# A hand-scheduled spectral + GLU kernel: the planner's assumed durations and two lags are changed, and with them the order of instructions

## Chip, cores, metric

One core of one Trainium2 chip. The metric is the device time of one launch in microseconds; the span in a profile is about 1.8 us shorter. Kernels are compared only within the same rounds. "Faster" or "slower" is said of a change over 2%.

## The reference, cut to what matters

```python
x  = A_x                              # 2048 rows of 512, bf16
xn = layernorm(x)
A  = irfft2(rfft2(xn) * (w_r + 1j*w_i))          # a spectral filter over both axes
B  = (gelu(xn @ w_gate) * (xn @ w_up)) @ w_down  # 512 -> 1792 -> 512
return x + A + B
```

## The kernel before

Everything is bf16 matmuls on TensorE. The spectral branch is written as small products with cosine and sine tables, threaded between the gate and up products of the GLU branch:

- rows come in 16 chunks of 128; VectorE takes statistics, GpSimd raises variance + eps to the power −1/2 (`rstd`), VectorE normalises (`xn`), a DMA transposes (`xnT`);
- four *folds*, one for each group of 4 chunks: VectorE forms sums and differences (`A`, then `xf`), TensorE does the first spectral products `bp` with `RF_t`, ScalarE copies them out;
- `dp`, `ep`: the next two spectral products; VectorE filters (`X`, `m`, `Y`, `F`); DMAs move the filtered block between partitions (`F2`); `gp`, `yp`: the products back;
- `g_ps`, `u_ps`: gate and up products, 14 pairs for each of four row blocks (the first in pieces); `ge` is the gelu on ScalarE, `hT` the product of the two on VectorE; `yp__n`: down products.

The order on each engine is not written by hand. A small list scheduler is told for each operation its engine, an assumed duration, its inputs, a priority and a *lag*: how much later than the input's end a reader on another engine may be placed. From that it makes one order, and the program is issued in it:

```python
at = max([d.end + (0.0 if d.eng == o.eng and not d.nbytes else d.lag + self.HOP)
          for d in o.deps if d.eng != "PE" or o.eng != "PE"] + [0.0])
# ... cut
r = add("POOL", 0.55, lambda: nc.gpsimd.tensor_tensor(          # the power, for n chunks at once
    out=rstd[:, k], in0=ve[:, k], in1=half[:, k], op=ALU.pow), (e, o_mem[1]), due - 5, lag=0.1)
# ... cut: then n normalisations on VectorE, each planned at 0.04 + 0.29
a2 = dve(0.61, f2, (a0, a1), t, new=(xb,), use=(ab,))
a3 = dve(0.61, f3, (a2,), t, use=(ab, xb))                      # the last step of a fold
# ... cut
p = pe(0.222, mm, (a2, a3, d_rf), t + 1, new=(sb,), use=(xb,))  # bp
```

At run time each engine is given its instructions in that order and waits on semaphores. An assumed number therefore costs nothing in itself. It decides who stands in front of whom. That this matters on TensorE the trace of the kernel before shows: when a `bp` came 0.48 us late, at 36.01, no `g_ps` or `u_ps` from behind it ran in that time (the next one starts at 36.69).

## Time and profile before

| | before |
|---|---|
| median of the first 3 runs | 180.46 us (180.26 to 180.72) |
| span of the profiled run | 178.8 us |
| TensorE busy | 97% |
| VectorE, ScalarE busy | 67%, 48% |
| TensorE starts behind its pace, 32 us to the end | 1.98 us |

The last row is not on the page. In the timeline a matmul overlaps the next (four that start 0.86 us from the next four are shown as 1.03), and a row can hide a wait (the eight `gp` at 84.34 are one row without idle time, and 0.16 us late), so an engine that is "97% busy" may still be late. Take the timeline, subtract start from start, and compare with the pace (0.86 us for four matmuls of 512 columns, 0.22 for four of 128). What is over is a *hold*. The prediction shows the lines.

### The profile page before, as it was taken

What the parts mean: (1) busy time and instruction counts of PE and PEld (TensorE: products, weight loads), DVE (VectorE), ACT (ScalarE), POOL (GpSimd) and SP (SyncE); (2) the same over time, 40 slices, a digit from 0 to 9 for tenths busy, and PEclk for the clock granted to TensorE, in tenths of its full rate; (3) what the DMA queues carried; (4) which work ended last, traced back from release to release, by engine and by line L of the source; (5) the groups of instructions that cost most, each with busy time, mean ns of one, the idle gap of its engine ahead of it and who ended that gap; (6) DMA issues with size and microseconds to landing.
All of it is one profiled execution on the core that took longest, in us unless ns stands there. A gap on an engine that the chain in (4) does not pass through costs nothing.

```text
span 178.8 us, 3152 instructions
## 1 busy us (share of the span) xinstructions
PE 173.8 (97%) x1154; PEld 98.8 (55%) x1154; DVE 120.0 (67%) x268; ACT 86.1 (48%) x156; POOL 16.7 (9%) x33
## 2 busy tenths in 40 slices
PE   6999999999999999999999999999999999999993
PEld 2798898554455544445555545555445444544463
DVE  2589899999952556999999999730941642633522
ACT  3224273364678965469999997454311211211100
POOL 3210112007870000000000000000000000000000
DMA  5999953268959700013111221110041221222212
GB/s 159 325 355 257 335 109 61 61 186 212 228 148 356 227 0 0 0 45 74 48 44 31 59 62 47 45 27 4 5 142 60 88 92 59 88 69 78 73 48 59
DMA packets 23215, 19.51 MB, mean 109 GB/s; under 512 B 9568, under 2 KB 21856, under 8 KB 23200
## 3 DMA queue, kind: packets, MB, share of 16 engines
q1 hardware_dynamic: 22464, 17.84, 36.8%
q0 software_dynamic: 320, 1.19, 2.5%
q10 hardware_dynamic: 416, 0.30, 0.5%
q8 instruction: 9, 0.15, 0.3%
q14 instruction: 6, 0.05, 0.1%
HBM read 13.28 MB, written 2.10 MB: 86 GB/s over the span
## 4 chain that ended last, share of the span: by engine, by line
PE 85%; DVE 9%; issue 2%; ACT 2%; POOL 1%; DVEq 0%; POOLq 0%
PE u_ps L508 22%; PE g_ps L508 22%; DVE hT L533 3%; PE warm L387 3%; PE yp L827 2%; PE bp L590 2%; PE yp__2106 L881 2%; PE yp__2079 L881 2%; PE yp__2048 L881 2%; PE yp__1963 L881 2%; PE yp__1932 L881 2%; PE yp__1905 L881 2%; PE yp__1874 L881 2%; PE yp__1788 L881 2%; PE yp__1750 L881 2%
## 5 line engine op out<-in xcount | busy, mean ns | idle before, releaser
L508 PE MATMUL g_ps<-xnT,Wg_sb 128*128 128x512 bf16 (+2 forms) x296 | 58.1, 330 | 0.0
L508 PE MATMUL u_ps<-xnT,Wu_sb 128*128 128x512 bf16 (+2 forms) x296 | 57.7, 327 | 0.1
L525 ACT ACTIVATE ge<-g_ps 128x512 bf16<-128x512 f32 x56 | 33.6, 600 | 36.6 <-PE g_ps L508 33.1
L533 DVE TENSOR_TENSOR hT<-u_ps,ge 128x512 bf16<-128x512 f32 x56 | 38.4, 685 | 14.0 <-PE u_ps L508 13.9
L508 PEld LDWEIGHTS <-Wg_sb 128*128 128x128 bf16 x296 | 27.7, 99 | 18.8 <-issue 0.4
L508 PEld LDWEIGHTS <-Wu_sb 128*128 128x128 bf16 x296 | 27.3, 98 | 19.4 <-issue 0.8
L881 PEld LDWEIGHTS <-hT 128*128 128x128 bf16 x252 | 23.0, 98 | 21.9
L833 ACT CAST yf<-yp 128x512 bf16<-128x512 f32 x16 | 9.1, 590 | 36.3 <-PE yp L827 36.3
L661 ACT CAST E<-ep 64x512 bf16<-64x512 f32 x32 | 18.6, 581 | 0.9 <-PE ep L655 0.5
L403 DVE BATCH_NORM_STATS2 st<-x_t 128x6 f32<-128x512 bf16 x16 | 10.8, 676 | 4.1 <-DMA x_t<-in_A_x_dram 4.1
L638 ACT CAST ds<-dp 128x512 bf16<-128x512 f32 x16 | 9.0, 589 | 1.1 <-PE dp L633 1.0
L417 POOL TENSOR_TENSOR rstd<-ve,half 128x2 f32<-128x2 f32 (+2 forms) x7 | 6.0, 857 | 33.8 <-DVE ve L411 33.8
L782 ACT CAST Gs<-gp 128x512 bf16<-128x512 f32 x16 | 8.7, 596 | 0.7 <-PE gp L776 0.7
L594 ACT CAST Bs<-bp 128x512 bf16<-128x512 f32 x16 | 8.4, 599 | 0.6 <-PE bp L590 0.6
L423 DVE TENSOR_SCALAR xn<-x_t,mv,rstd 128x512 bf16<-128x512 bf16 (+1 forms) x18 | 6.5, 407 | 0.8 <-POOL rstd L417 0.8
L849 DVE TENSOR_TENSOR lv<-yf 128x512 bf16<-128x512 bf16 x8 | 3.4, 425 | 4.9 <-ACT yf L833 4.0
L827 PEld LDWEIGHTS <-Gs 128*128 128x128 bf16 x64 | 4.7, 98 | 3.1
L387 PE MATMUL warm<-warm 128*128 128x512 bf16 (+1 forms) x12 | 4.9, 579 | 1.3 <-POOL half L380 1.3
L827 PE MATMUL yp<-CT,Gs 128*128 128x128 bf16 x64 | 5.7, 219 | 0.0
L633 PEld LDWEIGHTS <-Bs 128*128 128x128 bf16 x64 | 4.4, 98 | 2.2
L692 DVE TENSOR_TENSOR m<-X,TW 128x1024 bf16<-128x1024 bf16 x8 | 5.5, 690 | 0.2
L776 PEld LDWEIGHTS <-F 128*128 128x128 bf16 x64 | 4.4, 98 | 2.1
(103 smaller groups left out, 170.1 us busy)
## 6 DMA issues: line engine op xcount, KB each, us to landing
y<-in_A_x_dram SPq DMA_DIRECT2D x16, 128.0 KB, 2.1
F<-F SPq DMA_DIRECT2D x32, 64.0 KB, 2.0
out_dram<-y SPq DMA_DIRECT2D x15, 128.0 KB, 1.7
Wd_sb<-in_B_w_down_dram SPq DMA_DIRECT2D x1, 1792.0 KB, 8.6
Wu_sb<-in_B_w_up_dram SPq DMA_DIRECT2D x3, 512.0 KB, 5.1
x_t<-in_A_x_dram SPq DMA_DIRECT2D x3, 512.0 KB, 8.2
Wg_sb<-in_B_w_gate_dram SPq DMA_DIRECT2D x2, 512.0 KB
Wg_sb<-in_B_w_gate_dram SPq DMA_DIRECT2D x2, 256.0 KB, 4.0
```

Source lines behind the costliest of these rows:

```text
L387: nc.tensor.matmul(tiles["warm"][:, 0:w], lhsT=warm[:, 0:P], rhs=warm[:, 0:w], start=True, stop=True)
L403: V.bn_stats(out=st[:], in_=x_t[:, c])
L508: nc.tensor.matmul(tiles[f"{nm}.{key}"][:, f * w:f * w + w], lhsT=W[:, e, (f0 + f) * P:(f0 + f + 1) * P], rhs=rhs(e), start=(f + e == 0), ...
L525: nc.scalar.activation(out=e[:, 0:nf * w], in_=tiles[f"g_ps.{key}"][:, 0:nf * w], func=AF.Gelu_apprx_tanh)
L533: V.tensor_tensor(out=out, in0=tiles[f"u_ps.{key}"][:, 0:nf * w].rearrange("p (f w) -> p f w", w=w) if nf > 1 else tiles[f"u_ps.{key}"][:, ...
L594: nc.scalar.copy(out=o, in_=tiles[f"bp.{cg}.{q}"][:].rearrange("p c (r g a) -> p (c r) g a", r=2, a=4))
L638: nc.scalar.copy(out=ds[:].rearrange("p (s k t) -> p s k t", s=2, t=2), in_=tiles[f"dp.{G}"][:].rearrange("p s t k -> p s k t"))
L661: nc.scalar.copy(out=tiles[f"E.{g}"][64 * h:64 * h + 64, r], in_=tiles[f"ep.{g}.{h}"][64 * r:64 * r + 64])
L782: nc.scalar.copy(out=o, in_=tiles[f"gp.{g}.{h}"][:].rearrange("p q (n a) -> p (q n) a", a=4))
L827: nc.tensor.matmul(yp[:, q], lhsT=tiles["G"][:, q, c], rhs=IQ[q], start=(q == 0), stop=(q == 3), skip_group_check=True)
L833: nc.scalar.copy(out=tiles[f"yf.{c // 2}"][:, c % 2], in_=tiles[f"yp.{c}"][:])
L881: nc.tensor.matmul(y[:, s], lhsT=tiles[sb, f][:, cl * P:(cl + 1) * P], rhs=Wd_sb[:, f, s], start=(f == 0), stop=False)
```

## The change

The intent: the planner believed that all powers take 0.55 us; those of four chunks take longer (1.38 us in the trace of before). And it placed first spectral products, and the products of filtered blocks, too close behind their inputs. The whole diff:

```diff
-        r = add("POOL", 0.55, lambda: nc.gpsimd.tensor_tensor(
+        r = add("POOL", 0.28 + 0.275 * n, lambda: nc.gpsimd.tensor_tensor(
...
-                XN[c].append(dve(0.04 + 0.29 / halves, lambda c=c, d=d: V.tensor_scalar(
+                XN[c].append(dve(0.06 + 0.29 / halves, lambda c=c, d=d: V.tensor_scalar(
...
         a3 = dve(0.61, f3, (a2,), t, use=(ab, xb))
+        a3.lag = 1.2
...
-                ex.append(dma(64 * 1024, mv_, [last] + ex[:1], t, new=(f2,) if not ex else (), use=(fb, f2), lag=0.5,
+                ex.append(dma(64 * 1024, mv_, [last] + ex[:1], t, new=(f2,) if not ex else (), use=(fb, f2), lag=1.0,
```

Below, *part 1* is the two assumed durations, *part 2* the lag of 1.2 behind the fold, *part 3* the lag of 1.0 behind the move of a filtered block.

## The prediction

> **What bounds the kernel now.** I read the totals first, then TensorE's waits, then its timeline for the places where it starts late, then the engine that ended each of those waits.
>
> ```profile
> span 178.8 us, 3152 instructions
> PE 173.8 (97%) x1154; PEld 98.8 (55%) x1154; DVE 120.0 (67%) x268; ACT 86.1 (48%) x156; POOL 16.7 (9%) x33
> ```
>
> TensorE is busy nearly all the time. [...] a short hold can hide inside "busy"; what counts is the distance between starts. The next view is TensorE's timeline: start, duration, line, shapes, count, idle time before it.
>
> ```profile
> 34.45 1.03 PE L508 MATMUL g_ps<-xnT,Wg_sb 128*128 128x512 bf16 x4
> 35.31 0.39 PE L590 MATMUL bp<-RF_t,xf 128*128 128x128 bf16 x4
> 36.01 0.84 PE L590 MATMUL bp<-RF_t,xf 128*128 128x128 bf16 x12 [0.31 <-DVE xf L576]
> ...
> 42.74 1.03 PE L508 MATMUL g_ps<-xnT,Wg_sb 128*128 128x512 bf16 x4
> 43.91 1.02 PE L508 MATMUL u_ps<-xnT,Wu_sb 128*128 128x512 bf16 x4
> 44.77 1.03 PE L508 MATMUL g_ps<-xnT,Wg_sb 128*128 128x512 bf16 x4
> 46.04 0.40 PE L590 MATMUL bp<-RF_t,xf 128*128 128x128 bf16 x4 [0.24 <-DVE xf L572]
> 46.64 0.84 PE L590 MATMUL bp<-RF_t,xf 128*128 128x128 bf16 x12 [0.20 <-issue]
> ...
> 84.34 0.77 PE L776 MATMUL gp<-CT,F 128*128 128x128 bf16 x8
> 84.95 1.03 PE L508 MATMUL g_ps<-xnT,Wg_sb 128*128 128x512 bf16 x4
> ...
> 102.52 1.03 PE L508 MATMUL g_ps<-xnT,Wg_sb 128*128 128x512 bf16 x4
> 103.64 0.38 PE L655 MATMUL ep<-ds,CT 128*128 128x512 bf16 x1
> ```
>
> Four 512-column matmuls take 0.86 us from start to start (34.45 to 35.31), four 128-column ones 0.22. Against that pace the late starts are: bp at 36.01 by 0.48; u_ps at 43.91 by 0.31; bp at 46.04 by 0.40 and at 46.64 by 0.37; inside the eight gp at 84.34 (0.61 to the next group where 0.45 is the pace) 0.16; ep at 103.64 by 0.26. Together 1.98 us. Earlier there are 0.12 (first g_ps of the third and fourth chunks, 19.52) and 0.08 (first bp, 23.10). Everything else between 7.5 us and the last matmul runs at pace. So the end is set by TensorE's total work plus these holds, and about 2 us (1.1%) is all that any reordering can get.
>
> The holds of the folded products come from VectorE and GpSimd:
>
> ```profile
> 40.52 1.38 POOL L417 TENSOR_TENSOR rstd<-ve,half 128x4 f32<-128x4 f32 x1 [9.11 <-DVE ve L411]
> ```
> ```profile
> 35.27 0.68 DVE L576 TENSOR_TENSOR xf<-A 128x1024 bf16<-128x1024 bf16 x1
> ...
> 41.94 1.33 DVE L423 TENSOR_SCALAR xn<-x_t,mv,rstd 128x512 bf16<-128x512 bf16 x3 [0.30 <-POOL rstd L417]
> 43.19 0.67 DVE L533 TENSOR_TENSOR hT<-u_ps,ge 128x512 bf16<-128x512 f32 x1
> ...
> 45.31 0.68 DVE L572 TENSOR_TENSOR xf<-A 128x1024 bf16<-128x1024 bf16 x1
> 45.91 0.68 DVE L576 TENSOR_TENSOR xf<-A 128x1024 bf16<-128x1024 bf16 x1
> ```
>
> The last fold of group 1 ends at 35.95, and bp waits for it. The power of four columns took 1.38 us where the plan has 0.55, so the normalisation began late, the hT behind it at 43.19 freed its u_ps buffer late (the hold at 43.91), and the fold of group 2 ended at 46.59 (the holds at 46.04 and 46.64).
>
> [...] during the 0.48 us at 36.01 no g_ps or u_ps behind the bp ran, so order decides. [...]
>
> **The change part by part.** No instruction is added, removed or resized; only numbers in the list scheduler that fixes each engine's order change. Compared instruction by instruction, the orders differ so:
>
> 1. Power 0.28 + 0.275n instead of 0.55, normalise 0.06 + 0.29 instead of 0.04 + 0.29. For n = 4 that is 1.38, as measured. VectorE's order changes from the second pair of chunks on: more statistics and hT come ahead of the normalisations.
> 2. A lag of 1.2 behind the last fold. The bp of group 1 now stands behind the second u_ps of block 1 instead of ahead of it; that of group 2 behind the eighth g_ps instead of the seventh; that of group 3 one up/gate pair further too.
> 3. A lag of 1.0 instead of 0.5 behind the move of filtered blocks. Most gp, dp and ep stand one gate or up further back; the last eight gp come behind two down-projection blocks.
>
> Cost of 1 and 2, laid out by hand with start-to-start times from this trace: hT, A, xf, statistics 0.60; an xf that needs the A just before it 0.71; statistics to its aggregate 0.70; normalise 0.32. TensorE's groups at pace.
>
> Early: chunks 4 and 5 are normalised at about 23.2 instead of 21.96, chunks 6 and 7 at 26.05 instead of 25.49. The last transposing DMA of the block moves from 27.19 to about 27.75; with the 3.0 us median landing it is there at 30.8, and block 1 starts at 32.7. No hold.
>
> Group 1: A at 30.88, four normalises from 31.48, hT between, xf at 33.36 and 34.56, end 35.24. TensorE: g_ps, u_ps, g_ps, u_ps from 32.72, so bp is due at 36.18, 0.9 us later than its input. The 0.48 is gone. The u_ps before it (35.31) needs the hT that ends at 34.65; good.
>
> Group 2: aggregates done at 39.5, power 39.9 to 41.3, hT at 39.64, both A at 40.24 and 40.84 beside the power, hT 41.44, normalises from 42.04, hT at 43.0, xf 43.92 and 44.52, end 45.2. TensorE reaches u_ps number 6 and 7 at 43.1 and 44.85, needing hT ends of 42.1 and 43.7, and bp at 46.6. The 0.31, 0.40 and 0.37 are gone.
>
> Group 3: xf end 49.1, bp due at 50.95. Good. Sum of 1 and 2: 0.48 + 0.31 + 0.40 + 0.37 = 1.56 us.
>
> From there dp starts at 54.44 (54.42 before): the spectral chain keeps its clock time, and TensorE has one gate/up pair (1.73 us) more behind it, which is the 1.56 seen from the other side.
>
> Cost of 3: the four ep at 77.79 come at about 76.97. ScalarE then works without pause through eight E copies (0.60 each), two gelu and the ds copies, as before from 78.05; now from about 77.8, because the gelu ahead of it stays. Its first ds copy ends at about 84.3. The third dp (due 81.74) needs the bank of the sixth E copy (free about 81.9), and the second gp (due 83.91) that of the first ds copy: holds of 0.15 and then to 0.45 in all, in place of 0.16. Further on I lay ScalarE's copies against the four S banks and find slack of 0.2 us and more; the hold of 0.26 at ep is gone, since that ep stands behind dp's copy by more than 5 us. VectorE's hT stand over 1 us ahead of the u_ps that need their buffers.
>
> Tail: four down blocks are open before the first inverse product, and the third needs the second pair's four VectorE steps. In the trace of before these end 4.56 us after the first yp starts (123.55 to 128.11); in the new order the product comes 4.79 us after it. It just fits; I charge 0.1.
>
> Sum: 1.98 removed, 0.45 and 0.1 put back, so about 1.4 us: 180.46 − 1.4 = 179.1 us.
>
> **Rivals.** *Nothing comes of it:* the bubbles move into the ScalarE-bound stretch from 77 to 108 us, where ScalarE is 97% busy and a TensorE that is 1.7 us ahead only waits for banks. For it: the 0.16 and 0.26 are just such waits. Against it: there are gate and up products to fill with, which only need gelu and hT. It would give 180 to 180.5. *Full gain:* no hold returns, 178.5. *Worse:* the postponed last gp and the four open blocks make the inverse products wait on copies and VectorE, 1 us or more per missed slot, 180.5 to 182. Against it: gp of the last block is due at 124.2 while its moved inputs should be there near 118.5. *A late transpose* holds block 1 at 32.7: margin 1.9 us, unlikely.
>
> **Range and chances.** 178.5 if all holds go, 180.3 if most come back; the three timings of before spread 0.46 us. So 178.3 to 180.3 at 8 in 10. A gain over 2% (under 176.9) exceeds all that the holds amount to: 1%. Slower by over 2% needs 5 us of new holds: 1%.
>
> **What would show it.** Right: no idle before bp near 36.2, 46.6 and 51; no late u_ps between 37 and 47; dp first at 54.4; TensorE's last down product some 1.4 us earlier. The new holds at dp and gp near 82 to 84.5 behind ScalarE copies, a few tenths. Wrong: a late first g_ps of block 1, late yp_ products (line 885 before) near 132, or holds at ep and dp from 90 to 106 that sum to over 1 us.

From the text on record a clause and most of a paragraph are cut, at the marks, because they do not rest on a trace of this case; what its traces show of it stands in this document with its number. Its sum: 1.98 removed, 0.45 and 0.1 put back, so 1.43.

## The result, and the profile after

After: 179.19 us median (178.68 to 179.40, 6 runs); before, beside it: 180.43 us (180.14 to 180.72, 6 runs). The ratio is 0.9924, interval 0.9905 to 0.9943. A ratio here is the mean time of one kernel's runs over that of the other's of the same rounds, so it is not quite the ratio of the two medians. By the 2% rule the two are the same; the gain of about 0.8% is clear of the noise.

The totals of the changed kernel:

```profile
span 176.9 us, 3153 instructions
PE 172.1 (97%) x1154; PEld 98.1 (55%) x1154; DVE 118.8 (67%) x268; ACT 85.7 (48%) x156; POOL 17.4 (10%) x33
```

The same 1154 matmuls, the same 97%: the page alone would not tell what happened. TensorE's timeline does. These are the places where the kernel before was held (columns: start, duration, engine, line, operation, tiles, shapes, count, and in brackets idle time, where there is any):

```profile
35.09 1.03 PE L508 MATMUL u_ps<-xnT,Wu_sb 128*128 128x512 bf16 x4
35.96 1.06 PE L591 MATMUL bp<-RF_t,xf 128*128 128x128 bf16 x16
36.85 1.03 PE L508 MATMUL g_ps<-xnT,Wg_sb 128*128 128x512 bf16 x4
...
45.48 1.03 PE L508 MATMUL g_ps<-xnT,Wg_sb 128*128 128x512 bf16 x4
46.35 1.06 PE L591 MATMUL bp<-RF_t,xf 128*128 128x128 bf16 x16
...
83.41 0.87 PE L777 MATMUL gp<-CT,F 128*128 128x128 bf16 x8
84.12 1.03 PE L508 MATMUL u_ps<-xnT,Wu_sb 128*128 128x512 bf16 x4
```

The 16 `bp` of group 1 stand behind the second `u_ps` now, run as one row of 0.89 us, and nothing is late before or after; those of group 2 the same. The one hold left after 32 us is inside the eight `gp`: 83.41 to 84.12 is 0.71, where the pace is 0.45, so about 0.27.

VectorE, for the two groups:

```profile
33.89 0.68 DVE L576 TENSOR_TENSOR xf<-A 128x1024 bf16<-128x1024 bf16 x1
...
44.00 0.68 DVE L576 TENSOR_TENSOR xf<-A 128x1024 bf16<-128x1024 bf16 x1
```

The last `xf` of group 1 ends at 34.57, that of group 2 at 44.68 (before: 35.95 and 46.59), 1.4 and 1.7 us ahead of the `bp`.

Where did the time come from? Split the span at two marks: the first 512-column `g_ps`, where row block 1 begins, and the last matmul. First the two lines of the kernel before, then those of the changed one:

```profile
32.72 0.59 PE L508 MATMUL g_ps<-xnT,Wg_sb 128*128 128x512 bf16 x2
...
175.92 0.22 PE L885 MATMUL yp__2188<-yt,RI_t 128*128 128x128 bf16 x1
```
```profile
32.51 1.03 PE L508 MATMUL g_ps<-xnT,Wg_sb 128*128 128x512 bf16 x4
...
173.97 0.22 PE L886 MATMUL yp__2188<-yt,RI_t 128*128 128x128 bf16 x1
```

From mark to mark: 143.20 us before, 141.47 after (unrounded times), so 1.73 us less. From the last matmul to the end of the span: 2.92 and 2.93. Up to the first mark: 32.72 and 32.51, and that piece will turn out to vary from run to run.

### The profile page after: what moved, and what is told of

Read it like the earlier page. It is cut to its first block, busy times and chain, and to the rows that moved or that the text cites. A ratio compares the mean times of both kernels' runs of the same rounds, so it can differ in the third digit from the quotient of the medians.

```text
span 176.9 us, 3153 instructions
## 1 busy us (share of the span) xinstructions
PE 172.1 (97%) x1154; PEld 98.1 (55%) x1154; DVE 118.8 (67%) x268; ACT 85.7 (48%) x156; POOL 17.4 (10%) x33
## 4 chain that ended last, share of the span: by engine, by line
PE 92%; DMA 3%; ACT 2%; SPq 1%; issue 0%; DVE 0%
PE u_ps L508 27%; PE g_ps L508 26%; DMA Wu_sb<-in_B_w_up_dram 3%; PE yp L828 2%; PE bp L591 2%; PE gp L777 2%; PE ep L656 2%; PE dp L634 2%; PE yp__2106 L882 2%; PE yp__2079 L882 2%; PE yp__1990 L882 2%; PE yp__1963 L882 2%; PE yp__1932 L882 2%; PE yp__1902 L882 2%; PE yp__1716 L882 2%; PE yp__2132 L882 2%
## 5 line engine op out<-in xcount | busy, mean ns | idle before, releaser
L417 POOL TENSOR_TENSOR rstd<-ve,half 128x2 f32<-128x2 f32 (+2 forms) x7 | 5.6, 805 | 32.5 <-DVE ve L411 32.5
L387 PE MATMUL warm<-warm 128*128 128x512 bf16 (+1 forms) x12 | 4.3, 514 | 1.3 <-POOL half L380 1.3
```

## The experiments

The theory: the end is TensorE's work plus its holds, and the four holds of groups 1 and 2 came from VectorE's order, made with too short a power, and from `bp` that stood too close. The open questions: which part of the change removes them, is the power the cause at all, does the last hold mean that ScalarE sets a pace, and why do the two traces differ by 1.94 us when the medians differ by 1.24?

All eleven runs in one table, below the two kernels themselves. "Block 1" is the first mark; "rest" is from there to the last matmul; "holds" are those after the first mark, by the timeline. Where figures are joined by +, the first is that of groups 1 and 2. Each row has one trace, of one launch, while the median is of 4 to 6 launches.

| run | median us | ratio to before (interval) | block 1 | rest | holds after block 1 |
|---|---|---|---|---|---|
| before | 180.43 | 1 | 32.72 | 143.20 | 1.98 |
| changed | 179.19 | 0.9924 (0.9905 to 0.9943) | 32.51 | 141.47 | 0.27 |
| changed, again | 178.81 | 0.9904 (0.9883 to 0.9925) | 32.67 | 141.46 | 0.27 |
| changed, third | 178.97 | 0.9909 (0.9895 to 0.9922) | 33.38 | 141.47 | 0.27 |
| part 1 alone | 179.25 | 0.9928 (0.9902 to 0.9954) | 33.21 | 141.53 | 0.27 |
| part 2 alone | 179.35 | 0.9938 (0.9916 to 0.9960) | 32.66 | 141.83 | 0.36 + 0.28 |
| part 3 alone | 180.60 | 1.0000 (0.9975 to 1.0025) | 33.16 | 142.80 | 1.20 + 0.38 |
| parts 1 and 2 | 178.81 | 0.9908 (0.9893 to 0.9923) | 32.55 | 141.46 | 0.27 |
| before, cheap power | 179.60 | 0.9947 (0.9932 to 0.9963) | 32.96 | 142.00 | 0.40 + 0.15 + 0.25 |
| before, power twice | 183.96 | 1.0185 (1.0170 to 1.0201) | 35.00 | 145.44 | 3.80 + 0.42 |
| changed, power twice | 179.94 | 0.9968 (0.9952 to 0.9983) | 33.87 | 141.48 | 0.27 |
| changed, half of gp back | 179.13 | 0.9923 (0.9909 to 0.9936) | 33.18 | 141.20 | none |
| changed, gp back, table first | 178.52 | 0.9896 (0.9881 to 0.9911) | 32.40 | 141.20 | none |

The kernel before, as the neighbour of these runs, had medians of 180.41, 180.54 and 180.53. Four traces (changed again, parts 1, 2 and 3 alone) lack 16 or 17 of the 1154 matmul records; each shows as a start exactly one matmul late and is not counted as a hold.

### The changed kernel once more, twice

No edit.

> The changed kernel, unchanged, once more. Theory (the gain is the removed holds of TensorE, and the two traces differ by more than the medians only because of the first 8 us, which vary from run to run): again one hold in the trace after 32 us, 0.2 to 0.35 us inside the first eight gp near 84; time 179.0 to 179.4. Rival (the trace was a lucky one and other runs have holds in the middle): holds between 36 and 110 us that sum to 0.5 us or more.

> The changed kernel, as the neighbour of the next two on the same chip. From the first g_ps of block 1 to the last matmul 141.4 to 141.5 us in the trace as twice before; the start of block 1 anywhere from 32.5 to 33.3 us; time 178.8 to 179.4.

The rest is 141.46, 141.47 and 141.47 us in three traces, with the same hold of 0.27 at `gp`. The start of block 1 was 32.51, 32.67 and 33.38, the last a little over what was expected; the median of the second (178.81) lies a little under its 179.0 to 179.4. So in this kernel everything behind the first mark repeats to 0.01 us, and the noise of the medians is made in front of it. In the third trace the first `g_ps` of chunks 2 and 3 is late by 0.56 at 19.8 and the first `bp` by 0.50 at 23.8; in the first there is neither. These two wait for transposed chunks and for the table `RF_t`, both brought by DMA (landed at 19.63 and 23.71). The theory holds; the first pair of traces was one of the longer runs of before (180.62) beside the fastest of after (178.68), and overstates the gain.

### Part 1 alone: the two assumed durations

```diff
-        r = add("POOL", 0.55, ...
+        r = add("POOL", 0.28 + 0.275 * n, ...
-                XN[c].append(dve(0.04 + 0.29 / halves, ...
+                XN[c].append(dve(0.06 + 0.29 / halves, ...
```

> The kernel before with only the two assumed durations changed (power 0.28 + 0.275n, normalise 0.06 + 0.29). VectorE's order up to the second folded group is then that of the changed kernel, while the bp stand where they stood before (group 1 behind the second g_ps, due 35.1; group 2 behind the seventh u_ps, due 45.5). Theory (VectorE's order is what removes the holds; the lag only adds a reserve): xf of the two groups ends near 34.6 and 44.7, all four holds are gone, 179.0 to 179.5. Rival (the lag behind the fold, bp further back, is what removes them): holds stay at the bp near 36 and 46, 179.9 to 180.5.

TensorE at the two groups:

```profile
35.80 1.06 PE L590 MATMUL bp<-RF_t,xf 128*128 128x128 bf16 x16
...
45.32 1.03 PE L508 MATMUL u_ps<-xnT,Wu_sb 128*128 128x512 bf16 x4
46.19 1.06 PE L590 MATMUL bp<-RF_t,xf 128*128 128x128 bf16 x16
```

All four holds are gone. The theory's number came out (rest 141.53, time 179.25), the rival's did not. In group 1 `bp` stands in its old place, so `bp` further back is not needed there. In group 2 it does not, though my expectation says so: it stood behind the seventh `g_ps` and now stands behind the seventh `u_ps`, 0.86 us further back. By estimate the old place would have done there too: its first four and the rest would have been due at 45.33 and 45.55, and in this trace the two `xf` ended at 44.79 and 45.39. No run shows it. Nor were the two durations run apart. Built but not run, the kernel before with only the 0.06 already places that `bp` behind the seventh `u_ps`; with only the new power it does not.

### Part 2 alone: the lag behind the fold

```diff
         a3 = dve(0.61, f3, (a2,), t, use=(ab, xb))
+        a3.lag = 1.2
```

> The kernel before with only the lag of 1.2 behind the last fold. The bp stand as in the changed kernel, VectorE's order up to the second group is nearly that of before. Theory (VectorE's order): the 0.48, 0.40 and 0.37 at bp are gone, but the sixth u_ps, due 43.1, waits for the hT behind the late normalisation until about 43.8: a hold of 0.5 to 0.9 comes in place of 0.31; early net gain about 0.8. The order from 68 us on is quite another (ep and dp come earlier), so 179.3 to 180.2 in all. Rival (the lag does it all): no hold between 36 and 48, 179.0 to 179.3.

TensorE (first fence) and VectorE (second) of this run:

```profile
42.19 1.03 PE L508 MATMUL g_ps<-xnT,Wg_sb 128*128 128x512 bf16 x4
43.41 1.02 PE L508 MATMUL u_ps<-xnT,Wu_sb 128*128 128x512 bf16 x4 [0.20 <-issue]
```
```profile
42.69 0.67 DVE L533 TENSOR_TENSOR hT<-u_ps,ge 128x512 bf16<-128x512 f32 x1
```

The `hT` behind the late normalisation ends at 43.36, and the `u_ps` that takes over its buffer starts at 43.41 instead of 43.05: 0.36. (The bracket counts only idle time after the shown end, and names no engine; the time of the `hT` tells.) The hold that the theory foresaw is there, but smaller than the 0.5 to 0.9 that I expected: I had taken VectorE's times from the trace of before, and with `bp` out of the way that `hT` ran 0.5 us earlier (43.19 before). A second hold of 0.28 came at an `ep` at 75.8, in an order that is quite different from 68 us on. So either part alone brings most of the gain. They are two answers to the same four holds and do not add up.

### Part 3 alone, and everything without it

```diff
-  ... use=(fb, f2), lag=0.5,
+  ... use=(fb, f2), lag=1.0,
```

> The kernel before with only the lag of 1.0 behind the move of the filtered blocks. Up to 80 us its order is that of before. Theory: the four holds of 1.56 us in all between 36 and 47 are as before, those at gp and ep (0.16 and 0.26) may go or change by a few tenths: 179.9 to 180.6, same as before within 0.3%. Rival (the filtered blocks' lag brings a good part of the gain): 179.7 or less, with the holds at gp and ep gone.

> The changed kernel without the lag of 1.0 behind the move of the filtered blocks (powers and fold's lag alone). Theory (that lag brings nothing here): the order is the same up to 96 us; from the first g_ps of block 1 to the last matmul 141.4 to 141.7 us, with the one hold of 0.27 at the first gp; same time as the changed kernel within 0.3 us. Rival (the lag of the filtered blocks keeps holds away later on): holds of 0.3 us or more between 96 and 125 us.

Alone it gains nothing (ratio 1.0000): the holds of groups 1 and 2 stay (0.12 + 0.31 + 0.40 + 0.37), and the 0.16 and 0.26 give way to one of 0.38 at an `ep`. The first hold is shorter because block 1 began 0.44 us later in this trace while the `xf` ended only 0.08 later (36.04): here the hold of the old order swallowed most of the late start. The last matmul came at 175.96, against 175.92 in the trace of before. In the changed kernel, which has no hold there, the start of 33.38 instead of 32.51 moved the last matmul by all of its 0.87, from 173.97 to 174.85. So a launch that starts late should gain less than 1.73. Left out of the change, it is not missed: 141.46 us and the one hold of 0.27. Part 3 brought nothing here.

### A cheap power in the old order

```diff
-            out=rstd[:, k], in0=ve[:, k], in1=half[:, k], op=ALU.pow), ...
+            out=rstd[:, k], in0=ve[:, k], in1=half[:, k], op=ALU.mult), ...
```

Its output is wrong, which doesn't matter for the time.

> The order of the kernel before, with GpSimd multiplying in place of raising to a power (wrong result on purpose). The four-column instruction should fall from 1.38 to some 0.4 us (the trace has 0.37 for another small one). The normalisations then start behind the hT ahead of them, 0.37 us earlier in each group. Theory (true power longer than planned, in VectorE's order of before, causes the holds): the hold at the first late bp falls from 0.48 to 0.1 to 0.2, the 0.31 at u_ps goes, and of the 0.40 and 0.37 at the second bp most stays, since that bp is reached earlier too; gain 0.5 to 1.0 us: 179.4 to 179.9. Rival (the power's length is beside the point): all four holds as before, 180.2 to 180.6.

GpSimd, then TensorE at group 2:

```profile
40.06 0.57 POOL L417 TENSOR_TENSOR rstd<-ve,half 128x4 f32<-128x4 f32 x1 [9.51 <-DVE ve L411]
```
```profile
45.07 0.39 PE L590 MATMUL bp<-RF_t,xf 128*128 128x128 bf16 x4
45.70 0.84 PE L590 MATMUL bp<-RF_t,xf 128*128 128x128 bf16 x12 [0.24 <-DVE xf L576]
```

With 0.57 us, which happens to be what the old plan assumed, the holds at the first `bp` and at `u_ps` are gone; of the two at the second `bp` one of 0.40 stays. Rest 142.00 instead of 143.20. So the power's true length made about 1.2 of the 1.6 us; the other 0.4 stayed, at a `bp` that stands close behind its input. I had expected a little less of the first. Block 1 began 0.23 us later in this trace than in that of before, which by itself shortens the first hold, so a part of the 1.2 may be that.

### Twice the power, in the old and in the new order

```diff
-        r = add("POOL", ..., lambda: nc.gpsimd.tensor_tensor(...), ...)
+        r = add("POOL", ..., lambda: [nc.gpsimd.tensor_tensor(...) for _ in range(2)], ...)
```

> The order of the kernel before, with each power done twice in a row (the result stays right). Two four-column powers take 2.76 us. Theory: the normalisation of group 1 starts 1.4 us later and with it bp; the same again for group 2. Holds between 32 and 48 us of 1.56 + 2.2 to 2.8, so 182.5 to 183.3. Rival (the power's length is beside the point): 180.4 to 180.8.

> The order of the changed kernel, with each power done twice in a row. Theory (the new order holds a reserve between the normalisation and the bp): the xf of group 1 end 1.2 us later, near 35.8, just ahead of bp's turn at 36.0; the second u_ps may wait 0.1 to 0.3 for the hT behind the late normalisation; group 2 likewise just fits. So at most 0.1 to 0.4 us more than the changed kernel: 178.9 to 179.6. Rival (the new order is as exposed to the power as the old): 181 or more.

TensorE in the old order, then the same stretch in the new one:

```profile
35.00 1.03 PE L508 MATMUL g_ps<-xnT,Wg_sb 128*128 128x512 bf16 x4
36.92 1.02 PE L508 MATMUL u_ps<-xnT,Wu_sb 128*128 128x512 bf16 x4 [0.89 <-DVE hT L533]
...
46.17 1.03 PE L508 MATMUL g_ps<-xnT,Wg_sb 128*128 128x512 bf16 x4
48.43 1.02 PE L508 MATMUL u_ps<-xnT,Wu_sb 128*128 128x512 bf16 x4 [1.23 <-DVE hT L533]
```
```profile
35.60 1.03 PE L508 MATMUL g_ps<-xnT,Wg_sb 128*128 128x512 bf16 x4
36.46 1.03 PE L508 MATMUL u_ps<-xnT,Wu_sb 128*128 128x512 bf16 x4
37.32 1.06 PE L591 MATMUL bp<-RF_t,xf 128*128 128x128 bf16 x16
38.22 1.03 PE L508 MATMUL g_ps<-xnT,Wg_sb 128*128 128x512 bf16 x4
```

A pair of four-column powers took 2.47 us in the old order, both times, and 2.58 and 2.59 in the new one, where I had expected 2.76. In the old order `u_ps` is late by 1.05 and 1.39, and the rest grows by 2.24 us to 145.44, within the 2.2 to 2.8 expected. In the new order it stays at 141.48: not one hold more. This is what the change bought: the new order has slack for the 1.2 and 1.6 us that a second power adds in groups 1 and 2; the last `xf` still end 0.67 and 0.44 us ahead of `bp`. This slack is that of the whole change: with part 1 alone `bp` starts only 0.53 and 0.80 us behind the last `xf`, and that order was not run with two powers. Both launch times lie above what I expected (183.96 and 179.94), because I had forgotten the early powers. They delay the first chunks: the first `g_ps` starts at 7.45 instead of 6.47 in the old order, the first `bp` is late by 0.73 and 0.94, and block 1 begins at 35.00 and 33.87. The 35.00 is not typical: its launch took 185.14 us, the other four 183.77 to 183.98. In that trace the matmuls of 128 columns ran at 0.107 us each, about half their pace of 0.056, until 9.96 us; in the trace of before until 7.38. This does not touch the rest.

### The last hold

In the changed kernel, ScalarE's copies of `dp` just before the hold:

```profile
83.27 1.07 ACT L639 CAST ds<-dp 128x512 bf16<-128x512 f32 x2
```

The first of the two takes until 83.85, and the second half of `gp` starts at 83.90. The edit takes the order as the scheduler made it and moves one entry:

```diff
     order = plan.run()
+    behind(("gp", 0, 1), ("u", 2, 11))   # second half of the first gp, behind the u_ps that follows it
```

> The changed kernel, with the second half of the first filtered block's products put behind the u_ps that follows it, 0.86 us later in TensorE's order; nothing else moves. Theory (the last hold, 0.27 near 83.9, is the wait for a PSUM bank that ScalarE's ds copy frees at 83.85): the hold is gone and no other comes, 0.27 less than the changed kernel beside it, 178.5 to 178.9. Rival (ScalarE sets the pace of this stretch): the hold comes back at the next ep or gp, the same time as the changed kernel.

```profile
84.09 0.39 PE L778 MATMUL gp<-CT,F 128*128 128x128 bf16 x4
84.31 1.03 PE L508 MATMUL u_ps<-xnT,Wu_sb 128*128 128x512 bf16 x4
85.17 0.39 PE L778 MATMUL gp<-CT,F 128*128 128x128 bf16 x4
```

The hold is gone and no other takes its place: 141.20 us, which is 0.27 less. The rival, that ScalarE paces this stretch, falls. The launch time did not show it: 179.13 (178.96 to 179.20) is above the 178.5 to 178.9 that I expected, and no launch of the changed kernel ran beside it. In the one launch that was traced, block 1 began at 33.18: two `u_ps` were late, by 0.43 at 11.5 and 0.72 at 15.7, the second until its up weights had landed at 15.64. Why the other four were as long is not shown.

### A version with two mends

```diff
+    behind(("gp", 0, 1), ("u", 2, 11))
             load_x(8, 4, 0.0, deps=XN[3], prio=-80.0)      # moved behind the load of RF_t
```

> Two mends on the changed kernel: the second half of the first filtered block's products one place back (as tried), and the table of the first spectral products loaded ahead of the third quarter of x instead of behind it. Theory: from block 1 to the last matmul 141.2 us, and no wait of the first bp near 23 us (it was 0.08 to 0.94 us in some traces, none in others), so 0.3 to 0.5 us less than the changed kernel beside it: 178.4 to 178.8. Rival (the early waits only move to another transfer, such as the up weights): the same time as the changed kernel less 0.2 at most.

178.52 us (178.33 to 178.81), ratio to before 0.9896, as expected. The rest is 141.20 and the first `bp` waits for nothing. It is the fastest version told here, but against the changed kernel the lead is not clear of noise: beside it (178.97) the median is 0.45 us less, and the single launches overlap (178.57 to 179.55 there). By the traces 0.27 of that is the hold. What the earlier table brings is not shown by one trace, because the changed kernel also had traces without a wait there, and the intervals of the two ratios overlap.

## Why the prediction was right

*The bound.* Predicted: TensorE's work plus holds, at most 2 us to gain. Shown: with no hold the rest is 141.20 us, and 143.20 − 141.20 is 2.00, against the 1.98 summed from starts.

*Parts 1 and 2, 1.56 us.* Right, to the place: no hold at `bp` or `u_ps` between 32 and 50 us. Laid out by hand, the last `xf` were to end at 35.24 and 45.2 and `bp` to start at 36.18 and 46.6; measured 34.57, 44.68, 35.96 and 46.35. Some of the shift is block 1 beginning 0.21 earlier. `dp` was to start at 54.44 and started at 54.18. The 54.42 that I set beside it was misread: it is from the view of the critical chain, which puts TensorE's starts 0.16 later than the timeline (54.26 there). Against the timeline `dp` was forecast 0.18 later, which, taken off the gate/up pair's 1.73, gives the 1.55. The prediction gave 1 and 2 one joint sum and did not say that each alone would nearly do; the single-part runs showed that.

*Group 2's power.* I used 1.38 us; in the new order it took 1.01. The margin was larger than laid out; nothing depended on it.

*Part 3, and the stretch from 77 us.* The mechanism was right (a `gp` waits for the bank of the first `ds` copy), the size was not: 0.45 predicted, 0.27 measured. The first `ds` copy was to end at 84.3 and ended at 83.85, since ScalarE's eight copies began at 77.38, not 77.8. The first copy starts 0.49 us after the start of its gelu (76.89), where I had allowed 0.60: that is 0.11 of the 0.42. Where the rest of my 77.8 came from, the prediction's working does not show. The hold of 0.15 at the third `dp` did not come. The 0.26 at `ep` went, as said; but since the order of parts 1 and 2 without part 3 loses it too, it is not part 3 that removed it.

*The tail, 0.1 us.* Nothing was lost. The VectorE steps end 4.55 us after the first `yp` and the product comes 4.79 us after it, as laid out.

*The sum.* 1.43 predicted behind the first mark, 1.73 measured there. The 1.2 to 1.6 us of the three pairs of medians are that gain with the early, run-to-run part on both sides; that late starts cost the old order less (see part 3 alone) may be why none reaches 1.73, but only one trace of the kernel before was kept. 179.1 predicted; 179.19, 178.81 and 178.97 measured. That the first agrees to 0.1 us is in part luck: 0.3 us more than forecast came off behind the mark, and the spread in front of it was not in the sum. The last matmul came 1.95 us earlier in the traces, not 1.4. The rival "nothing comes of it" (ScalarE was 96% busy in its stretch, 29.87 of 31 us in the trace of before, not 97%) is refuted by the run without any hold, and "late transpose" did not happen: the last one landed at 30.34, for use at 32.5.

## What to carry to other kernels

Read holds from the distance between starts, at the places where small products wait for another engine; a busy share of 97%, before and after, says nothing about them. Where a planner fixes the order, a wrong duration of a small instruction can hold an engine that never touches it: here a power of 1.38 us, planned at 0.55, and some 1.2 us of holds on TensorE that went with the cheap one (a part of it may be that trace's later start). An order has enough reserve behind an instruction when making that instruction longer no longer moves the work behind it, and doubling it in both orders tests just that. Look at the stretch in question, and not only at the launch: here the early powers, doubled too, still moved the end.

## What the runs showed that I had not expected

- The four-column power took 1.38 us in one place and 1.01 us in another of the same run (group 1 and group 2 of the new order; 1.38 twice in the old order); with the powers doubled it also took 1.12 and 1.50. The cause is not shown, nor how exact these spans are.
- Behind the first 33 us, three traces of one kernel agree to 0.01 us in 141; the 0.87 us between the launches that were traced (178.68, 178.83, 179.55) is all in front of that mark (32.51, 32.67, 33.38). A mend of 0.3 us behind the mark is better judged on the trace than on the launch time.
- Part 2 alone made `hT` run half a microsecond earlier (start 42.69, not 43.19). Here taking a hold away moved the producer too, and a hold laid out from the old trace at 0.5 to 0.9 us came out at 0.36.

## Further times measured

- Streams of weight load and matmul in the changed kernel (its page counts 1154 loads for 1154 matmuls): sixteen of 128 columns in 0.89 us (35.96 to 36.85), eleven times four of 512 in 9.50 us (36.85 to 46.35), so about 56 and 216 ns from start to start.
- On VectorE, in the changed kernel, an operation that reads what the one just before it wrote starts 0.72 us after it (46.96 to 47.68), and one that need not wait 0.60 us after it (46.36 to 46.96):

```profile
46.36 0.68 DVE L564 TENSOR_TENSOR A<-xn 128x1024 bf16<-128x1024 bf16 x1
46.96 0.68 DVE L568 TENSOR_TENSOR A<-xn 128x1024 bf16<-128x1024 bf16 x1
47.68 0.69 DVE L572 TENSOR_TENSOR xf<-A 128x1024 bf16<-128x1024 bf16 x1
```

- On GpSimd, on 128 partitions in fp32: the power took 0.70 us for 2 columns and 1.38 or 1.01 for 4, a multiply in its place 0.19 and 0.57.
